# Attention outputs of one unit: written into the output product's PSUM banks instead of the score tiles

## The chip, the cores and the metric

The kernel runs on one core of a Trainium2 chip. The time is device microseconds of one execution, so lower is better. Five engines matter: PE (TensorE: matmuls, and PEld for its weight loads), DVE (VectorE), ACT (ScalarE), POOL (GpSimd) and SP (SyncE, which here only issues DMAs). Each works through its own queue in order and waits on semaphores that the others raise.

## The reference

Attention over 8 batches, 12 heads, 448 positions and a head size of 64, with one more term in the softmax's denominator, followed by a two-layer product whose activation is Mish:

```python
def _attn_ref(q, k, v):
    scale = 1.0 / np.sqrt(q.shape[-1])
    scores = scale * np.matmul(q, k.transpose(0, 1, 3, 2))
    m = np.max(scores, axis=-1, keepdims=True)
    e = np.exp(scores - m)
    attn = e / (np.sum(e, axis=-1, keepdims=True) + np.exp(-m) + 1e-09)
    return np.matmul(attn, v)

def _moe_ref(x, w_in, w_out):          # x: 3584 x 768, w_in: 768 x 2048, w_out: 2048 x 768
    h = x @ w_in
    return (h * np.tanh(np.log1p(np.exp(h)))) @ w_out
```

`x` is the attention output with the heads side by side. The reference guards the exponential for h over 20.

## The kernel before

**Pairs and units.** Heads are handled in pairs: 6 pairs to a batch (`HP`), 48 in all. Three pairs make a unit (`UNIT_PAIRS`), two units a batch, so there are 16 units, numbered from 0. Batch 0 (units 0 and 1) runs through a loop of its own; then one loop goes over units 2 to 19, of which 2 to 15 have attention work. The instructions are put into the engines' queues in exactly the order in which this code calls them.

**A unit of the main loop** has two stages. In the first, twelve steps (numbered 0 to 11, four for each of three pairs) each call `exps` for the scores of this step, then `flush_late`, then some *filler*, then `scores_ahead`. From unit 4 on the filler is the output product (`mm2_part`, line 446) of earlier batches, cut into chunks of two matmuls; the list `weight` says which share of it each step gets (5.2 for the first, 1 for eight, 0.4 for three). In the second stage the input product (`mm1_mish`, line 382) makes eight tiles of 128 hidden columns; between them stand, for the next unit, three groups of transposes of q and k (line 179), their copies out of PSUM (line 210 on DVE for q, into `qd`; line 218 on ACT for k), the sums' reciprocal (lines 296, 300), the multiplies that normalise the three pairs (line 317 on DVE, line 315 on POOL for the third), and the first three score steps.

**Scores.** Seven tiles of 128 query rows make a pair, two to a step, so a pair's steps 0 to 2 do two score matmuls (line 249), one DVE maximum over both banks (line 270, 128 x 896) and two ACT exponentials (line 283), and step 3 does one of each. A score tile has two banks; there are three such tiles, used in turn, so a step's scores wait for the exponentials of three steps before. In step 3 the second bank of the tile is unused.

**Attention outputs.** The normalised exponentials `en` are turned by a DMA transpose (line 321, issued by SP) into `eT`. `av_pair` (line 358) then makes a pair's output with eight matmuls of 112 x 64 weights, accumulated in one bank, and puts a copy into `xT` (line 367) on the list `late`; `flush_late` issues it. The input product of a batch reads `xT`. In units 4 to 15 the three outputs of the unit before are made by `scores`, at step 3 of each pair, in the unused bank of the step's own score tile: `av_with` names the pair, and `bank=sc[:, 1, :]` the place. The output's matmuls so stand just ahead of the step's one score matmul.

**The other banks.** Two single banks, `mo0` and `mo1`, are handed out by `mo_take` and come back when their content has been copied. The output product uses them part by part (384 or 192 columns of 128 rows, sixteen matmuls), its copy to `o_sb` (line 433) is also on `late`; the input product uses them tile by tile, in turn with one bank of the first score tile, and a bank is free when Mish (line 388) has read it.

**What is loaded when.** SP issues the loads of q, k and v, the transposes and the stores of the result; POOL issues the loads of `w_in_sb` and `w_out_sb` (line 148, the last four in unit 4) between its casts of q, k and v (lines 162 to 164).

The step loop, as far as the change touches it:

```python
            exps(idx)
            ...
            flush_late()
            acc += weight[n]
            want = int(total * acc / sum(weight) + 1e-6)
            while done < want:
                fn, w = filler.popleft()
                fn()
                done += w
            scores_ahead(end)
```

Of the kernel before, what the change touches and what calls it, by code (L numbers as in the profile page):

```python
# [15 lines left out]
UNIT_PAIRS = 3  # L16
# [3 lines left out]
def kernel(  # L20
# [28 lines left out]
    STEPS = 4  # L49
# [47 lines left out]
    ]  # L97

    loaded, casted, qkT, att, xT, gT, o_sbs, stats = {}, {}, {}, {}, {}, {}, {}, {}
    av_with, mids = {}, {}  # L100
    late = deque()

    def flush_late():
# [125 lines left out]
    def scores(idx):  # L229

        p, s = divmod(idx, STEPS)
        if s == 0:
            if p < HP or p % UNIT_PAIRS == 0:
                for nm in ("negm", "sums", "expm", "den", "rden"):
                    stats[nm] = st_pool.tile([128, UNIT_PAIRS, NTILE], FP32, tag=nm, name=nm)
            at = 0 if p < HP else p % UNIT_PAIRS
            att[p] = {nm: t[:, at, :] for nm, t in stats.items()}
            att[p].update(en=en_bufs[p % N_EN], whole=dict(stats))
        st = att[p]
        qT, kT = qkT[p]  # L240
        kA, kB = kT[0:64, :], kT[64:128, :]
        sc = sc_tiles[idx % len(sc_tiles)]
        if s == STEPS - 1 and p in av_with:
            av_pair(av_with.pop(p), bank=sc[:, 1, :])
        if p >= DIAG_FROM:
            cols = tuple(range(2 * s, min(2 * s + 2, NTILE)))
            negm = st["negm"][:, cols[0] : cols[-1] + 1]
            for bk, i in enumerate(cols):
                nc.tensor.matmul(  # L249
                    sc[:, bk, 0:S], lhsT=qT[:, i].rearrange("d h r -> d (h r)"), rhs=kT,  # L250
                    start=True, stop=True,
                )
        elif s < 3:
            qa, qb = 128 * s, 64 + 128 * s
            nc.tensor.matmul(  # L255
                sc[:, 0, 0:S], lhsT=qT[0:64, qa : qa + 128], rhs=kA, start=True, stop=True
            )
            nc.tensor.matmul(
                sc[:, 1, 0:S], lhsT=qT[64:128, qb : qb + 128], rhs=kB, start=True, stop=True
            )  # L260
            cols, negm = (s, 4 + s), st["negm"][:, s : s + 5 : 4]
        else:
            nc.tensor.matmul(
                sc[0:64, 0, 0:S], lhsT=qT[0:64, 384:S], rhs=kA, start=True, stop=True
            )
            nc.tensor.matmul(
                sc[64:128, 0, 0:S], lhsT=qT[64:128, 0:64], rhs=kB, start=True, stop=True
            )
            cols, negm = (3,), st["negm"][:, 3:4]
        nc.vector.tensor_reduce(  # L270
            out=negm, in_=sc[:, 0 : len(cols), 0:S], axis=AX.X, op=ALU.max, negate=True
        )
        st["sc", s] = (sc, cols)
# [67 lines left out]

        late.append(evac)

    def av_pair(p, act=False, bank=None):
        b, hp = p // HP, p % HP
        eT = att[p]["eT"]
        v_bf = casted[p][2]
        if b not in xT:
            xT[b] = xT_pool.tile([128, DM_T, S], BF16, tag="xT", name="xT")
        av = mo_take() if bank is None else bank  # L350
        for j in range(NT):
            for h in range(2):
                if p >= DIAG_FROM:
                    by_h = eT[0:SP_, j, :].rearrange("c (i h r) -> c h i r", h=2, r=64)
                    e_h = by_h[:, h]
                else:
                    e_h = eT[0:SP_, j, h * S : (h + 1) * S]
                nc.tensor.matmul(  # L358
                    av[h * 64 : (h + 1) * 64, 0:S],
                    lhsT=v_bf[:, h, j * D : (j + 1) * D],  # L360
                    rhs=e_h,
                    start=(j == 0), stop=(j == NT - 1),
                )
        copy = nc.scalar.copy if act else nc.vector.tensor_copy

        def evac():
            copy(out=xT[b][:, hp, :], in_=av[:, 0:S])  # L367
            if bank is None:
                mo_free.append(av)

        late.append(evac)
        del att[p], casted[p], qkT[p]


    def mm1_mish(b, ff):
        if ff == 0:
# [90 lines left out]
    for g in range(B // 2):  # L467
        u0 = first_mm2 + 4 * g
        rest = plan.pop(u0, [])
        if g == 0:  # L470
            plan[u0] = [(0, i, 0, 2) for i in range(2)] + [(0, 2, 0, 1)]
            plan[u0 + 1] = [(0, 2, 1, 1)] + [(0, i, 2, 2) for i in range(3)]
        else:
            plan[u0] = rest + whole(g, 0) + [(g, 1, 0, 1)]
            plan[u0 + 1] = [(g, 1, 1, 1), (g, 1, 2, 2)] + whole(g, 2)
        plan[u0 + 2] = [(g, 4, 0, 2), (g, 4, 2, 1)] + whole(g, 3)
        plan[u0 + 3] = [(g, 4, 3, 1)] + whole(g, 5) + [(g, 6, 0, 2)]
        if g < B // 2 - 1:
            plan[u0 + 4] = [(g, 6, 2, 2)]
        else:  # L480
            plan[u0 + 3] += [(g, 6, 2, 2)]


    weight = [5.2] + [1.0] * (steps - STEPS) + [0.4] * (STEPS - 1)

    LEAD = UNIT_PAIRS + 1
    LOAD_AT = (0, 3, 6)
    HEAD = HP
# [50 lines left out]

    for u in range(UNITS_PER_B, N_UNITS + 2 * UNITS_PER_B):  # L540
        attn = u < N_UNITS
        filler = deque()
        for part in plan.get(u, []):
            filler.extend(mm2_part(*part))
        total, done, acc = sum(w for _, w in filler), 0, 0.0
        p0 = u * UNIT_PAIRS
        if attn and u >= first_mm2:
            av_with.update({p0 + i: p0 + i - UNIT_PAIRS for i in range(UNIT_PAIRS)})
        end = min((u + 1) * UNIT_PAIRS, N_PAIRS) * STEPS

        for n in range(steps):
            pi, s = divmod(n, STEPS)
            p, idx = p0 + pi, p0 * STEPS + n
            late_tp = u == UNITS_PER_B and n == STEPS
            if late_tp:
                transpose_pair(p0 + 2)
            exps(idx)
            if late_tp:
                evac_qk(p0 + 2)
            if u == UNITS_PER_B + 1:  # L560
                for part in TURN_AT[1].get(n, []):
                    turn_on_pe(*part)
# [8 lines that stand above are left out]
            if n in LOAD_AT:  # L571
                load_pair(p0 + LOAD_AT.index(n) + LEAD)
                cast_pair(p0 + LOAD_AT.index(n) + LEAD - 1)
            if u - UNITS_PER_B < len(AV_AT):
                early = AV_AT[u - UNITS_PER_B]
                if n in early:
                    av_pair(early[n])
                if u == UNITS_PER_B:
                    for part in TURN_AT[0].get(n, []):
                        turn_on_pe(*part)  # L580
            elif s == (2 if pi else 0) and N_PAIRS <= p < N_PAIRS + UNIT_PAIRS:
                av_pair(p - UNIT_PAIRS)
            if u - UNITS_PER_B < len(W_AT):
                load_w(W_AT[u - UNITS_PER_B].get(n, 0))
        assert done == total

        moe = u < N_UNITS + UNITS_PER_B
        b, w = (u - UNITS_PER_B) // UNITS_PER_B, u % UNITS_PER_B
        nxt = p0 + UNIT_PAIRS
        todo = sorted(range(p0, nxt), key=lambda p: p in BY_PE)  # L590
        for f in range(FF_U):
            if moe:
                mm1_mish(b, w * FF_U + f)
            if u == UNITS_PER_B and f in (2, 6):
                load_w(1)
            if not attn:
                continue
            if f == 0:
                denominators(att[p0]["whole"])
                normalise(todo[0], dma=todo[0] not in BY_PE)  # L600
            if f in (1, 3, 5):
                transpose_pair(nxt + f // 2, bank=f // 2 % 2)
                evac_qk(nxt + f // 2)
            if f == 4:
                scores_ahead(min(nxt * STEPS + 1, N_PAIRS * STEPS))
            if f >= FF_U - 2:
                scores_ahead(min(nxt * STEPS + f - FF_U + 4, N_PAIRS * STEPS))
            if f == 3:
                normalise(todo[1], dma=todo[1] not in BY_PE)
            if f == 4:  # L610
                normalise(todo[2], dma=todo[2] not in BY_PE, on_pool=True)
        if moe and w == UNITS_PER_B - 1:
            gather_mid(b)
# [32 lines left out]
```

## Time and profile before

| What | Value |
|---|---|
| median of 3 runs | 487.4 us (486.32 to 488.11) |
| the profiled execution | 486.33 us, of which the span from first to last instruction is 484.6 |
| mean granted TensorE clock | 0.996 of full speed |
| exponentials, line 283 | 336, 209.3 us of ACT, mean 636 ns |
| maxima, line 270 | 192, 182.5 us of DVE; 1085 ns over two banks, 623 ns over one |
| output product, line 446 | 1024 matmuls, 142.1 + 24.9 us of PE |
| input product, line 382 | 768 matmuls, 141.1 + 20.8 us of PE |
| attention outputs, line 358 | 384 matmuls, 34.1 us (288 in score tiles) + 15.0 us (96 in mo banks) of PE |
| their copies, line 367 | 36 from score tiles (DVE, mean 615 ns), 12 from mo banks |

Busy time of PE is the time in which at least one matmul is under way; matmuls follow each other in a pipeline, so a mean of 326 ns for 384 columns goes with a start every 0.1625 us. "Idle before, releaser" says how long an engine stood and which instruction's semaphore came last before it went on. In units 6 to 15 a unit takes 26.3 to 26.6 us.

### The profile page before, as it was taken

How to read it: one execution, taken by the hardware profiler on the slowest of the kernel's cores; microseconds unless marked ns; L12 is line 12 of the kernel's file. 1: busy time of each engine (PE TensorE's matmuls, PEld its weight loads, DVE VectorE, ACT ScalarE, POOL GpSimd, SP SyncE). 2: the span in 40 equal slices, each digit the busy share in tenths (PEclk: the TensorE clock that was granted, in tenths of full speed). 3: DMA queues.
4: the chain of work that ended last, by engine and by line, in shares of the span. 5: the costliest groups of instructions: out<-in, count | busy, mean ns of one | idle time of the engine just before them, and what ended most of it. 6: DMA issues, size and time to landing. Idle time of an engine off the chain costs nothing.

```text
span 484.6 us, 8804 instructions
## 1 busy us (share of the span) xinstructions
PE 448.3 (93%) x2992; PEld 249.0 (51%) x2992; DVE 347.1 (72%) x702; ACT 348.8 (72%) x906; POOL 160.6 (33%) x266
## 2 busy tenths in 40 slices
PE   4566897898999999999999999999999999999996
PEld 2222444455555555555555565555555555556563
DVE  4898987978688786878698887878687868420021
ACT  5989778879786988879797879788797979412300
POOL 4623157355413324353434232343435230300000
PEclk9999998999999999999999999999999999999999
DMA  8999999999999999898998989998989595771112
GB/s 231 199 214 227 243 191 234 221 201 237 182 234 270 203 205 203 226 195 234 191 258 169 237 169 211 203 222 222 179 242 198 155 186 124 147 148 32 34 41 90
DMA packets 209452, 92.19 MB, mean 190 GB/s; under 512 B 166272, under 2 KB 205952, under 8 KB 209408
## 3 DMA queue, kind: packets, MB, share of 16 engines
q1 hardware_dynamic: 201920, 85.35, 81.2%
q0 software_dynamic: 7488, 6.29, 9.0%
q8 instruction: 23, 0.38, 0.3%
q14 instruction: 21, 0.17, 0.1%
HBM read 45.61 MB, written 11.01 MB: 117 GB/s over the span
## 4 chain that ended last, share of the span: by engine, by line
PE 72%; DVE 12%; ACT 7%; DMA 5%; issue 2%; SPq 1%; POOL 0%; DVEq 0%; POOLq 0%
PE mo L446 25%; PE mo L382 24%; PE sc L249 8%; DVE negm L270 7%; ACT en L283 6%; PE sc L358 6%; PE sc L382 3%; PE sc L179 3%; DMA eT<-en 2%; DVE en L317 2%; DMA k_f<-in_k_dram 1%; PE mo L358 1%; DMA q_f<-in_q_dram 1%; PE sc L255 1%; DVE eT L336 1%
## 5 line engine op out<-in xcount | busy, mean ns | idle before, releaser
L283 ACT ACTIVATE en<-sc,negm 128x448 bf16<-128x448 f32 x336 | 209.3, 636 | 26.9 <-DVE negm L270 15.2
L270 DVE TENSOR_REDUCE negm<-sc 128x2 f32<-128x896 f32 x192 | 182.5, 970 | 52.6 <-PE sc L249 42.6
L446 PE MATMUL mo<-w_out_sb,gT 128*128 128x384 bf16 (+1 forms) x896 | 142.1, 303 | 0.0
L382 PE MATMUL mo<-xT,w_in_sb 128*128 128x448 bf16 x672 | 141.1, 352 | 1.0 <-DVE xT L367 0.9
L388 ACT ACTIVATE gT<-mo 128x448 bf16<-128x448 f32 x112 | 61.2, 547 | 77.4 <-PE mo L382 77.1
L446 PEld LDWEIGHTS <-gT 128*128 128x128 bf16 x896 | 84.0, 98 | 46.8 <-issue 1.3
L382 PEld LDWEIGHTS <-w_in_sb 128*128 128x128 bf16 x768 | 72.8, 98 | 63.6 <-issue 2.5
L315 POOL TENSOR_SCALAR en<-en,rden 128x448 bf16<-128x448 bf16 x98 | 61.4, 646 | 114.7 <-DVE rden L308 98.7
L249 PE MATMUL sc<-kT,qd 128*128 128x448 bf16 x252 | 71.5, 354 | 0.3 <-ACT en L283 0.2
L283 ACT ACTIVATION_READ_ACCUMULATOR en<-sc,negm 128x1 f32 x336 | 69.0, 205 | 0.0
L162 POOL CAST q_bf<-q_f 112x512 bf16<-112x512 f32 x47 | 28.9, 615 | 120.1 <-DMA q_f<-in_q_dram 110.5
L317 DVE TENSOR_SCALAR en<-en,rden 128x448 bf16<-128x448 bf16 x238 | 64.2, 343 | 0.9
L433 DVE COPY o_sb<-mo 128x384 f32<-128x384 f32 (+1 forms) x64 | 32.1, 502 | 41.7 <-PE mo L446 41.5
L249 PEld LDWEIGHTS <-qd 128*128 128x128 bf16 x252 | 24.5, 97 | 28.9 <-issue 13.5
L358 PE MATMUL sc<-eT,v_bf 112*64 112x448 bf16 x288 | 34.1, 357 | 3.5 <-ACT en L283 2.3
L164 POOL CAST v_bf<-v_f 112x512 bf16<-112x512 f32 x48 | 29.6, 616 | 16.4 <-DMA v_f<-in_v_dram 13.4
L358 PEld LDWEIGHTS <-v_bf 112*64 112x64 bf16 x384 | 20.9, 114 | 24.9 <-issue 16.9
L210 DVE TENSOR_SCALAR qd<-sc 64x448 bf16<-64x448 bf16 x72 | 27.8, 386 | 6.4 <-PE sc L179 5.9
L255 PE MATMUL sc<-kT,qd 64*128 64x448 bf16 x36 | 17.6, 509 | 15.6 <-ACT en L283 13.3
L163 POOL CAST k_bf<-k_f 112x512 bf16<-112x512 f32 x47 | 28.9, 614 | 8.2 <-DMA k_f<-in_k_dram 7.5
L446 PE MATMUL mo<-w_out_sb,mid 128*128 128x384 bf16 x128 | 24.9, 326 | 0.0
L179 PEld LDWEIGHTS <-q_bf 112*128 112x128 bf16 x192 | 14.5, 104 | 17.8 <-DVE q_bf L162 4.4
(50 smaller groups left out, 311.4 us busy)
## 6 DMA issues: line engine op xcount, KB each, us to landing
q_f<-in_q_dram SPq DMA_DIRECT2D x48, 224.0 KB, 4.9
k_f<-in_k_dram SPq DMA_DIRECT2D x48, 224.0 KB, 5.2
v_f<-in_v_dram SPq DMA_DIRECT2D x48, 224.0 KB, 5.5
w_in_sb<-in_moe_w_in_dram POOLq DMA_DIRECT2D x12, 256.0 KB, 5.8
w_out_sb<-in_moe_w_out_dram POOLq DMA_DIRECT2D x8, 384.0 KB, 8.1
out_dram<-o_sb SPq DMA_DIRECT2D x7, 336.0 KB, 3.4
out_dram<-o_sb SPq DMA_DIRECT2D x8, 288.0 KB, 4.1
out_dram<-o_sb SPq DMA_DIRECT2D x8, 240.0 KB, 3.2
```

The source lines that it names most:

```text
L164: nc.gpsimd.tensor_copy(out=v_bf, in_=v_f)
L179: nc.tensor.transpose(by_s[s][:, t * SP_ : (t + 1) * SP_], src[:, t].rearrange("p h d -> p (h d)"), ident[:SP_, :SP_],)
L249: nc.tensor.matmul(sc[:, bk, 0:S], lhsT=qT[:, i].rearrange("d h r -> d (h r)"), rhs=kT, start=True, stop=True,)
L270: nc.vector.tensor_reduce(out=negm, in_=sc[:, 0 : len(cols), 0:S], axis=AX.X, op=ALU.max, negate=True)
L283: nc.scalar.activation(out=st["en"][:, :, c, 0:SP_], in_=sc[:, bk, 0:S].rearrange("q (j c) -> q j c", j=NT), func=AF.Exp, bias=st["negm"][ ...
L315: nc.gpsimd.tensor_scalar(scalar2=1.0, op0=ALU.mult, op1=ALU.mult, **args)
L317: nc.vector.tensor_scalar(scalar2=None, op0=ALU.mult, **args)
L358: nc.tensor.matmul(av[h * 64 : (h + 1) * 64, 0:S], lhsT=v_bf[:, h, j * D : (j + 1) * D], rhs=e_h, start=(j == 0), stop=(j == NT - 1),)
L382: nc.tensor.matmul(h_ps[:, 0:S], lhsT=w_in_sb[:, dm, ff * 128 : (ff + 1) * 128], rhs=xT[b][:, dm, :], start=(dm == 0), stop=(dm == DM_T - 1),)
L388: nc.scalar.activation(out=gT[b][:, ff, :], in_=h_ps[:, 0:S], func=AF.Mish)
L433: nc.vector.tensor_copy(out=o_sb[:, cols], in_=st["o"][:, 0:n_cols])
L446: nc.tensor.matmul(st["o"][:, 0:n_cols], lhsT=src[:, ff, c0 : c0 + 128], rhs=w_out_sb[:, ff, cols], start=(ff == 0), stop=(ff == FF_T - 1),)
```

## The change

`av_with` and the `bank` argument go. From unit 4 on, in units with attention, the three outputs of the unit before are entries of the filler: each is inserted in the middle of the chunks of one of the unit's first three parts of 384 columns (an entry with weight 6, where a chunk of 384 columns has weight 2 and one of 192 columns weight 1), or stands at the end if there are fewer such parts, as in unit 4. `av_now` makes the output in a bank from `mo_take` and at once issues what is in `late`, its own copy included. In three places of the plan the part of 192 columns comes ahead of the others.

```diff
--- before.py
+++ after.py
@@ -97,7 +97,7 @@
     ]
 
     loaded, casted, qkT, att, xT, gT, o_sbs, stats = {}, {}, {}, {}, {}, {}, {}, {}
-    av_with, mids = {}, {}
+    mids = {}
     late = deque()
 
     def flush_late():
@@ -240,8 +240,6 @@
         qT, kT = qkT[p]
         kA, kB = kT[0:64, :], kT[64:128, :]
         sc = sc_tiles[idx % len(sc_tiles)]
-        if s == STEPS - 1 and p in av_with:
-            av_pair(av_with.pop(p), bank=sc[:, 1, :])
         if p >= DIAG_FROM:
             cols = tuple(range(2 * s, min(2 * s + 2, NTILE)))
             negm = st["negm"][:, cols[0] : cols[-1] + 1]
@@ -341,13 +339,13 @@
 
         late.append(evac)
 
-    def av_pair(p, act=False, bank=None):
+    def av_pair(p, act=False):
         b, hp = p // HP, p % HP
         eT = att[p]["eT"]
         v_bf = casted[p][2]
         if b not in xT:
             xT[b] = xT_pool.tile([128, DM_T, S], BF16, tag="xT", name="xT")
-        av = mo_take() if bank is None else bank
+        av = mo_take()
         for j in range(NT):
             for h in range(2):
                 if p >= DIAG_FROM:
@@ -365,12 +363,15 @@
 
         def evac():
             copy(out=xT[b][:, hp, :], in_=av[:, 0:S])
-            if bank is None:
-                mo_free.append(av)
+            mo_free.append(av)
 
         late.append(evac)
         del att[p], casted[p], qkT[p]
 
+
+    def av_now(p):
+        av_pair(p)
+        flush_late()
 
     def mm1_mish(b, ff):
         if ff == 0:
@@ -468,12 +469,12 @@
         u0 = first_mm2 + 4 * g
         rest = plan.pop(u0, [])
         if g == 0:
-            plan[u0] = [(0, i, 0, 2) for i in range(2)] + [(0, 2, 0, 1)]
+            plan[u0] = [(0, 2, 0, 1)] + [(0, i, 0, 2) for i in range(2)]
             plan[u0 + 1] = [(0, 2, 1, 1)] + [(0, i, 2, 2) for i in range(3)]
         else:
-            plan[u0] = rest + whole(g, 0) + [(g, 1, 0, 1)]
+            plan[u0] = [(g, 1, 0, 1)] + rest + whole(g, 0)
             plan[u0 + 1] = [(g, 1, 1, 1), (g, 1, 2, 2)] + whole(g, 2)
-        plan[u0 + 2] = [(g, 4, 0, 2), (g, 4, 2, 1)] + whole(g, 3)
+        plan[u0 + 2] = [(g, 4, 2, 1), (g, 4, 0, 2)] + whole(g, 3)
         plan[u0 + 3] = [(g, 4, 3, 1)] + whole(g, 5) + [(g, 6, 0, 2)]
         if g < B // 2 - 1:
             plan[u0 + 4] = [(g, 6, 2, 2)]
@@ -483,6 +484,7 @@
 
     weight = [5.2] + [1.0] * (steps - STEPS) + [0.4] * (STEPS - 1)
 
+    AV_WEIGHT = 6
     LEAD = UNIT_PAIRS + 1
     LOAD_AT = (0, 3, 6)
     HEAD = HP
@@ -539,13 +541,17 @@
 
     for u in range(UNITS_PER_B, N_UNITS + 2 * UNITS_PER_B):
         attn = u < N_UNITS
-        filler = deque()
+        p0 = u * UNIT_PAIRS
+        filler, avs = deque(), deque()
+        if attn and u >= first_mm2:
+            avs.extend((lambda p=p: av_now(p), AV_WEIGHT) for p in range(p0 - UNIT_PAIRS, p0))
         for part in plan.get(u, []):
-            filler.extend(mm2_part(*part))
+            chunks = mm2_part(*part)
+            if avs and part[3] == 2:
+                chunks.insert(len(chunks) // 2, avs.popleft())
+            filler.extend(chunks)
+        filler.extend(avs)
         total, done, acc = sum(w for _, w in filler), 0, 0.0
-        p0 = u * UNIT_PAIRS
-        if attn and u >= first_mm2:
-            av_with.update({p0 + i: p0 + i - UNIT_PAIRS for i in range(UNIT_PAIRS)})
         end = min((u + 1) * UNIT_PAIRS, N_PAIRS) * STEPS
 
         for n in range(steps):
```

With it the outputs stand in PE's queue, counted in units 5 to 15, after 24 matmuls of the output product; straight after score step 5; and two product matmuls after score step 9. In DVE's queue their copies stand ahead of the maxima of steps 3, 6 and 10, where before they stood behind those of steps 3, 7 and 11. In unit 4 they stand ahead of score step 3, straight after step 7, and ahead of step 11.

## The prediction

> **What bounds the kernel now.** I read the busy rows first, then the windows of the product stages, then the stage at 183.64 us instruction by instruction, then the landings of the transposes.
>
> ```profile
> PE 448.3 (93%) x2992; PEld 249.0 (51%) x2992; DVE 347.1 (72%) x702; ACT 348.8 (72%) x906; POOL 160.6 (33%) x266
> ```
>
> The mean hides three stages. Columns below: stretch, its length, then busy time of PE, PEld, DVE, ACT, POOL. Each stretch runs from a unit's first output-product matmul to its first input-product matmul.
>
> ```profile
> 183.64:198.59 14.95, 14.95 (x105) 8.46 (x104) 11.06 (x15) 13.77 (x39) 6.19 (x11) 1.00 1.06 250
> 128.94:144.93 15.99, 15.03 (x105) 8.47 (x104) 11.06 (x15) 13.77 (x39) 5.40 (x10) 1.00 1.10 222
> 102.41:117.54 15.13, 12.89 (x89) 7.25 (x88) 11.81 (x16) 13.83 (x41) 8.40 (x15) 1.00 1.04 228
> ```
>
> In unit 7 (183.64), and nearly so in all of units 6 to 15, PE is never idle; ACT is busy 13.77 of 14.95 us. Units 5 (128.94) and 4 (102.41) hold idle PE time. Who waits there (total, times, longest):
>
> ```profile
> ACT en L283 <- DVE xT L367: 8.7, 21, 1.5
> ...
> PE sc L358 <- ACT en L283: 2.3, 4, 0.8
> PE sc L358 <- DMA eT<-en: 1.0, 1, 1.0
> ```
>
> So the attention outputs cost ACT 8.7 us and PE 3.3 us, which looks like the gain on offer. The timeline of unit 7 shows what it is worth:
>
> ```profile
> 187.00 0.95 PE L358 MATMUL sc<-eT,v_bf 112*64 112x448 bf16 x8
> ...
> 188.89 0.62 DVE L367 CAST xT<-sc 128x448 bf16<-128x448 f32 x1
> ...
> 189.62 0.63 ACT L283 ACTIVATE en<-sc,negm 128x448 bf16<-128x448 f32 x1 [0.50 <-DVE xT L367]
> ...
> 199.46 0.63 ACT L283 ACTIVATE en<-sc,negm 128x448 bf16<-128x448 f32 x1
> ...
> 200.87 1.32 DVE L317 TENSOR_SCALAR en<-en,rden 128x448 bf16<-128x448 bf16 x5
> ...
> 201.60 0.54 ACT L388 ACTIVATE gT<-mo 128x448 bf16<-128x448 f32 x1
> ```
>
> The exponential of the shared score tile waits 0.50 for the output's drain, yet PE is paced by a longer chain: last exponential (199.46), sums and reciprocal, seven L317 multiplies, then the qd copy (202.59 to 203.37). PE's second group of transposes starts at 203.52 and needs that copy: a margin of 0.10 us with 0.04 for the hand-over. Likewise the first Mish (201.60 to 202.14) frees a bank that PE takes at 202.39, margin 0.20. If the last exponential comes over 0.1 us later, PE stops.
>
> **The change, part by part.**
>
> *Instructions.* 36 outputs (units 4 to 15) move: 8 matmuls, 8 weight loads, one 0.615 us drain each. None is added or removed on any engine; the drain stays on DVE. Cost 0 in work.
>
> *Entering and leaving an output on PE.* Start to start, the matmul before L358 takes 0.256 (187.00) or 0.278 (191.93) us instead of 0.163, and L358's last pair to the next matmul 0.285. The 0.278 includes a hand-over from ACT: the second and third outputs start 0.04 us after the exponential that frees their score tile. In a mo bank the wait is for an o_sb copy. Elsewhere the entry is 0.176 (160.65). Saving per unit: 0 to 0.2 us; I take 0.04. Leaving into a product row (unit 16, 428.65) costs the same 0.285.
>
> *The plan's order* (192-column parts first): the same parts, 0.0825 us per 192-column and 0.1625 per 384-column matmul. Nothing on the path; if its cover went, one hand-over of 0.04.
>
> *What the outputs now stand before.* The weight of 6 shares the outputs into the twelve steps. The first moves from 3.36 to 2.71 us after the unit's start, the second from 8.29 to 7.24, the third from 13.22 to 12.25. They used to stand before score steps 3, 7 and 11 (one matmul, one 0.62 us maximum); now the second stands before step 6 and the third before step 10 (two matmuls, a 1.08 us maximum), and DVE takes the drain ahead of that maximum. I follow unit 7 through the queues by hand. Durations from its rows: score pair to maximum 0.65, single 0.40; the next DVE instruction starts 1.00 after a double maximum, 0.54 after a single, 0.53 after an xT drain, 0.465 after an o_sb copy; maximum to exponential 0.034 (0.115 if another wait stands ahead); exponentials 0.61 apart (0.62 after a pause); a tile is free 0.77 after its last exponential starts. Start times in us from the unit's start:
>
> | | score 4, exp 4 | score 5, exp 5 | score 6, exp 6 | score 8, exp 8 | score 10, exp 10 | exp 11 |
> |---|---|---|---|---|---|---|
> | before | 5.09, 6.90 | 6.12, 8.36 | 7.15, 9.60 | 10.02, 11.83 | 12.08, 14.53 | 15.82 |
> | after | 5.42, 7.18 | 6.77, 8.53 | 8.12, 10.06 | 10.00, 11.92 | 13.13, 14.91 | 16.14 |
>
> Exp 3 gains (5.98 to 5.39) and exp 4 gives it back, because score 4 stands behind two more product matmuls. Maximum 6 waits for the second drain (8.42 to 8.95), so exp 6 starts at 10.06 and score 9 waits 0.10 on it. The third drain starts at 13.24, maximum 10 at 13.79, exp 10 at 14.91 and exp 11 at 16.14, 0.32 us late. Queued behind it: Mish (bank taken 0.12 late), multiplies, qd copy, second transposes. Less the margin of 0.10, PE stands 0.22 us per unit. With the entry at 0.176 everything shifts and it is 0.06. I take 0.22, since 0.256 is the entry of the first output in seven of these ten units. Ten units: +2.2 us, bounds −2.0 (all entries saved, ACT never last) and +3.2 (no margin).
>
> *Unit 4.* Its three outputs wait 0.8, 1.0 and 0.7 us for ACT; in mo banks they don't. The same steps put exp 11 at 14.62 instead of 15.99, so the unit's second transposes come 1.4 us earlier.
>
> *Unit 5* takes that away.
>
> ```profile
> 121.68 11.62 DMA eT<-en
> ```
>
> (from the chain of waits.) This transpose shares the DMA engines with the last w_out_sb loads, which POOL issues at 115 to 119 us and which land by 129.97; it lands at 133.30, and the first output waits for it. POOL issues these loads after casts that wait for their own loads, not for unit 4. Starting the transpose 1.4 earlier behind the same packets brings 0 to 1.4; I take 0.1. After it, PE now has 0.65 us more product left, and exp 11 comes 1.0 us later from there on (13.43 after that output against 12.45). The normalise row then decides:
>
> ```profile
> 147.21 2.87 DVE L317 TENSOR_SCALAR en<-en,rden 128x448 bf16<-128x448 bf16 x7
> ```
>
> Seven multiplies take 2.87 us here against 1.81 at 119.81, while POOL casts run from 147.77 to 149.70; PE's second transposes wait 0.80 for them. About 0.9 us later they overlap the casts less: 2.6 us. Net, these transposes come 0.6 us later than 150.83; bounds −1.4 and +1.0. [...]
>
> *DMA order and landings.* In unit 7 the three transposes land 2.8, 3.5 and 4.8 us before their outputs; 0.65 to 1.05 us earlier is covered. Without that cover each wait would be PE's.
>
> *Sum.* +2.2 +0.6 = +2.8 us on the profiled execution's 486.33 (span 484.6 and 1.73 around it): 489.1. That execution is the fastest of three; from the median of 487.4 the sum gives 490.2.
>
> **Rivals.** 0.5% is 2.4 us, about what these measurements can tell from no change; the bounds are 484.96 and 489.84.
>
> 1. *Faster: ACT is not the last.* If exp 11 comes no later than before, PE keeps its margin and loses its waits: 0.2 in ten units, 0.7 beyond that in the third outputs at 223, 276 and 329, and unit 4's 1.4: 4.1, so 483.3. For it: ACT loses 8.7 us of waits on drains. Against: ACT is idle only 1.2 us in unit 7, and the table has it pause 1.2 before exp 4 alone. It decides below a lag of 0.1.
>
> 2. *Within 0.5%.* Entries of 0.176 (+0.6 in ten units) and a landing 0.5 earlier in unit 5 (+0.2): 488.2. Table entries are good to about 0.1 us and the margin is 0.10, so this is near.
>
> 3. *Much slower: the two mo banks.* The third output takes the bank drained by the o_sb copy ending at 12.20, 0.05 before it. If DVE is 0.5 late there, score 10, exp 10 and exp 11 follow: +0.7 per unit, 494.4. For it: no slack in the table. Against: the copies are DVE's 0.55 us rows, with no POOL partner. [...]
>
> 4. *It moves, but nothing follows*, PE being full: 487.4.
>
> **How the numbers follow.** Forecast 0.42 and rival 3 0.08: slower 0.50. Rival 2 0.28 and rival 4 0.04: same 0.32. Rival 1: 0.18. The time is the forecast's, 490.2, its own range 489.8 to 491.8. The 8-in-10 range, with the unknown entries, margin and landing, reaches 485.5 to 492.5.
>
> **What would show it.** Right: the rows of ACT waiting for xT gone; ACT waiting for negm grown; in units 6 to 15 PE waits of 0.1 to 0.3 us at the second transposes (on qd) or the fourth input-product group (on a Mish); the unit period up from 26.4 to about 26.6. Unit 4's product stage near 13.5 us instead of 15.1; the first output of unit 5 still starting near 133.3, after a longer wait. Wrong: last exponentials no later than 15.8 after the unit's start, or a period under 26.4; or output waits on o_sb (rival 3).

## The result and the profile after

| | before | changed |
|---|---|---|
| median of 6 runs, us | 487.75 (486.32 to 489.06) | 492.14 (490.58 to 493.79) |
| profiled execution, us (span) | 486.33 (484.6) | 493.79 (492.0) |
| mean granted TensorE clock | 0.996 | 0.964 |

The ratio is 1.009, with a 95% interval of 1.0066 to 1.0113: slower, by 4.4 us between the medians, where 2.8 was forecast. The forecast's own range (489.8 to 491.8) ends 0.3 us below the 492.14; its wide one (485.5 to 492.5) takes it in. The profiled executions stand 7.4 us apart. From the starts of the units' stages in the two traces, that difference is made of:

| stretch | before, us | changed, us | difference |
|---|---|---|---|
| start to unit 4's first output product | 102.41 | 105.15 | +2.74 |
| from there to unit 6's first input product | 69.82 | 71.70 | +1.88 |
| nine units from there, to unit 15's first input product | 237.96 | 239.93 | +1.97 |
| the rest | 74.41 | 75.22 | +0.81 |

The first row isn't the change's: no output moves before unit 4. Every kernel of this document has the same code up to there, and this stretch takes 101.80 to 106.33 us in their fourteen traces; what spreads it isn't known. The clock rows of the two pages (40 slices of the span, tenths of full speed) differ in slices 4 to 6, but that doesn't explain it. First the kernel before:

```profile
PEclk9999998999999999999999999999999999999999
```

The changed kernel, with its busy row; slice 12 (135 to 148 us) will matter:

```profile
PE 452.6 (92%) x2992; PEld 247.4 (50%) x2992; DVE 350.5 (71%) x702; ACT 348.8 (71%) x906; POOL 161.6 (33%) x266
...
PEclk9996588999989999999999999999999999999999
```

The kernel before runs at half rate there as well. Eight matmuls of an output take it 1.71 us up to 62 us of the span and 0.95 from there on:

```profile
60.27 1.71 PE L358 MATMUL mo<-eT,v_bf 112*64 112x448 bf16 x8
...
62.40 0.95 PE L358 MATMUL mo<-eT,v_bf 112*64 112x448 bf16 x8
```

Its trace holds no record of the clock from before its first change to full rate at 62 us, and the row shows such a stretch as full. The changed kernel reached the full rate once before, from 37.1 to 40.5 us, so that its row shows the half rate behind it. Most of the difference between the mean clocks of 0.996 and 0.964 is this. Experiment 7's row is like the changed kernel's, and unit 4's first output product starts at 102.67 us.

The other three rows add up to 4.66 us, near the 4.4 of the medians. They too are one execution each, and the second is the least sure: in experiment 5, with no output moved, it is 68.41 us. The third is firm: 237.93 to 238.36 us in the three kernels with the outputs in the score tiles (before, experiment 5, the second of experiment 8), 239.59 to 239.94 in the four with all of them moved as here, unit 5 apart (the changed one, experiments 6 and 7, the first of 8). The windows of the changed kernel for units 7, 5 and 4, columns as in the prediction (the last three are granted clock, DMA share, GB/s):

```profile
188.43:203.45 15.02, 15.02 (x105) 8.33 (x104) 11.82 (x16) 13.36 (x39) 6.40 (x11) 1.00 1.06 250
130.96:150.15 19.19, 16.59 (x105) 8.73 (x103) 11.82 (x16) 13.46 (x39) 5.79 (x10) 0.91 1.10 230
105.15:118.71 13.56, 12.79 (x88) 6.76 (x87) 11.95 (x17) 13.30 (x39) 6.86 (x12) 1.00 0.93 216
```

Unit 4's stage is 1.57 us shorter, unit 5's 3.20 longer, with a granted clock of 0.91 where before it had 1.00. The waits of the changed kernel (total, times, longest):

```profile
ACT en L281 <- DVE negm L268: 32.7, 49, 4.0
...
PE mo L356 <- DMA eT<-en: 3.1, 2, 2.6
```

ACT's 8.7 us of waits for the outputs' copies are gone, and its wait for the maxima has grown from 15.2 to 32.7. ACT is as busy as before (348.8 us): it got its time back in one place and lost it in another. Unit 7 shows where, in the timeline of the changed kernel (start, length, engine, what; in brackets the idle time before it and its releaser):

```profile
195.85 1.09 DVE L268 TENSOR_REDUCE negm<-sc 128x2 f32<-128x896 f32 x1 [0.26 <-PE sc L247]
...
196.86 0.61 DVE L365 CAST xT<-mo 128x448 bf16<-128x448 f32 x1
...
197.39 2.78 DVE L268 TENSOR_REDUCE negm<-sc 128x2 f32<-128x896 f32 x3
...
203.35 0.63 ACT L281 ACTIVATE en<-sc,negm 128x448 bf16<-128x448 f32 x1 [0.34 <-DVE negm L268]
...
204.59 0.63 ACT L281 ACTIVATE en<-sc,negm 128x448 bf16<-128x448 f32 x1
```

The second output's copy (196.86) stands ahead of maximum 6. Counted from the unit's start at 188.43, the exponentials 4, 5, 6, 8, 10 and 11 start at 7.19, 8.55, 10.07, 11.92, 14.92 and 16.16; the prediction's table had 7.18, 8.53, 10.06, 11.92, 14.91 and 16.14.

### The profile page after: what moved, and what is told of

It reads as the page before. It is cut to its first block, busy times and chain, and to the rows that moved or that the text cites. A ratio compares the mean times of both kernels' runs of the same rounds, so it can differ in the third digit from the quotient of the medians.

```text
span 492.0 us, 8718 instructions
## 1 busy us (share of the span) xinstructions
PE 452.6 (92%) x2992; PEld 247.4 (50%) x2992; DVE 350.5 (71%) x702; ACT 348.8 (71%) x906; POOL 161.6 (33%) x266
## 4 chain that ended last, share of the span: by engine, by line
PE 73%; DVE 10%; DMA 7%; ACT 6%; issue 2%; SPq 1%; POOL 0%; DVEq 0%; POOLq 0%
PE mo L447 26%; PE mo L383 22%; PE sc L247 9%; PE mo L356 7%; ACT en L281 5%; DVE negm L268 4%; DMA eT<-en 4%; DVE en L315 3%; PE sc L179 3%; PE sc L383 3%; DMA k_f<-in_k_dram 1%; DMA q_f<-in_q_dram 1%; PE mo L330 1%; PE sc L253 1%; DVE xT L365 1%
## 5 line engine op out<-in xcount | busy, mean ns | idle before, releaser
L281 ACT ACTIVATE en<-sc,negm 128x448 bf16<-128x448 f32 x336 | 209.3, 637 | 34.2 <-DVE negm L268 32.7
L447 PEld LDWEIGHTS <-gT 128*128 128x128 bf16 x896 | 82.7, 98 | 49.5 <-issue 6.2
L315 DVE TENSOR_SCALAR en<-en,rden 128x448 bf16<-128x448 bf16 x238 | 64.4, 342 | 0.9
L434 DVE COPY o_sb<-mo 128x384 f32<-128x384 f32 (+1 forms) x64 | 32.1, 502 | 37.1 <-PE mo L447 36.6
L356 PE MATMUL mo<-eT,v_bf 112*64 112x448 bf16 x384 | 49.6, 385 | 3.1 <-DMA eT<-en 3.1
L365 DVE CAST xT<-mo 128x448 bf16<-128x448 f32 x45 | 27.8, 621 | 29.5 <-PE mo L356 29.0
L247 PEld LDWEIGHTS <-qd 128*128 128x128 bf16 x252 | 22.8, 98 | 26.6 <-issue 12.5
L356 PEld LDWEIGHTS <-v_bf 112*64 112x64 bf16 x384 | 19.0, 115 | 27.6 <-issue 18.1
```

What stands on the lines that cost most here:

```text
L247: nc.tensor.matmul(sc[:, bk, 0:S], lhsT=qT[:, i].rearrange("d h r -> d (h r)"), rhs=kT, start=True, stop=True,)
L281: nc.scalar.activation(out=st["en"][:, :, c, 0:SP_], in_=sc[:, bk, 0:S].rearrange("q (j c) -> q j c", j=NT), func=AF.Exp, bias=st["negm"][ ...
L315: nc.vector.tensor_scalar(scalar2=None, op0=ALU.mult, **args)
L356: nc.tensor.matmul(av[h * 64 : (h + 1) * 64, 0:S], lhsT=v_bf[:, h, j * D : (j + 1) * D], rhs=e_h, start=(j == 0), stop=(j == NT - 1),)
L434: nc.vector.tensor_copy(out=o_sb[:, cols], in_=st["o"][:, 0:n_cols])
L447: nc.tensor.matmul(st["o"][:, 0:n_cols], lhsT=src[:, ff, c0 : c0 + 128], rhs=w_out_sb[:, ff, cols], start=(ff == 0), stop=(ff == FF_T - 1),)
```

## The experiments

Each kernel was timed in five rounds beside the kernel before on the same chip; a ratio is to that. The runs with outputs at other places come first, then unit 5, then both together.

**1. Second and third outputs before single maxima.**

```diff
-                chunks.insert(len(chunks) // 2, avs.popleft())
+                at = len(chunks) // 2 if len(avs) == UNIT_PAIRS else 3 * len(chunks) // 4
+                chunks.insert(at, avs.popleft())
```

> The changed kernel with one thing moved: the second and third output of a unit stand after three quarters of their part instead of the middle, so that in units 5 to 15 they come straight before score steps 7 and 11 (one maximum of 0.62 us) and not before steps 6 and 10 (two banks, 1.08 us). Banks and early drains stay. Theory (the place in the score chain makes the exponentials late): the unit period goes from 26.6 back to about 26.4, the waits of 0.1 us on a Mish, on qd and of step 9 on ACT vanish, and the time falls by 10 x 0.24 = 2.4 us to 489.7. Rival (two banks are too few): the period stays at 26.6 and the time at 492.

489.4 us, ratio 1.0032 (1.0008 to 1.0055). The changed kernel's window of unit 7's output product is shown above (15.02 us); its input product's follows:

```profile
203.45:215.02 11.57, 11.57 (x79) 6.45 (x78) 9.37 (x27) 8.42 (x19) 3.29 (x6) 1.00 0.82 180
```

and both windows of unit 7 in this kernel:

```profile
188.01:202.92 14.91, 14.91 (x104) 8.34 (x103) 11.79 (x16) 13.60 (x39) 6.18 (x11) 1.00 1.05 247
202.92:214.33 11.41, 11.41 (x81) 6.46 (x79) 9.38 (x27) 7.99 (x19) 3.44 (x7) 1.00 0.86 193
```

The unit takes 26.32 us instead of 26.59. (Before: 14.95 and 11.40, 26.35.) The whole loss of the steady units is in the place of two outputs, and it splits as the prediction's two waits do: 0.11 in the first stage, 0.16 in the second.

**2. Third output alone.**

```diff
+                at = 3 * len(chunks) // 4 if len(avs) == 1 else len(chunks) // 2
+                chunks.insert(at, avs.popleft())
```

> The changed kernel with the third output of each unit alone at three quarters of its part (before a single maximum); the second stays in the middle, before a double one. The hand table of the prediction has the second output put exponential 8 only 0.09 us late and the third put exponential 11 0.32 late. Theory (it is the third whose place costs): the steady unit returns to 26.4 us and the time to about 490. Rival (the second output's place, which delays exponential 6, is the loss): 26.6 us a unit, 492.

489.42 us, ratio 1.004 (1.0017 to 1.0063). The same two windows of this kernel:

```profile
187.68:202.70 15.02, 15.02 (x105) 8.33 (x103) 11.82 (x16) 13.70 (x40) 6.39 (x11) 1.00 1.09 242
202.70:214.10 11.40, 11.40 (x79) 6.46 (x78) 9.38 (x27) 7.88 (x19) 3.28 (x6) 1.00 0.90 199
```

The second stage is back at 11.40, the first still 15.02. The unit takes the 26.42 us of the theory, but the loss has two parts: the third output's place costs the 0.17 of the input product (Mish and second transposes late), and the second output's place the 0.11 of the output product, where score step 9 waits for exponential 6.

**3. The banks without the places.** The kernel before with its outputs in the free bank, at their old places, first with the copy left on `late`, then drained at once.

```diff
-            av_pair(av_with.pop(p), bank=sc[:, 1, :])
+            av_pair(av_with.pop(p))
```

> The kernel before with the outputs at their old places but in mo banks instead of the score tiles, their copies issued a step later as before. Theory: the exponential of step 3, 7 and 11 no longer waits for the copy (ACT waiting for xT, 8.7 us, gone), but the next part wants the output's bank 0.65 to 1.0 us after the output, before the late copy has ended: PE waits 0.4 us twice and 0.8 once in a unit, some 1.6 x 11 = 18 us at most, 495 to 505. So new banks need the early copy. If banks cost nothing: 487 or less.

506.27 us, ratio 1.0385 (1.0361 to 1.0409), just above the 495 to 505 that were expected. Waits of this kernel:

```profile
PE mo L382 <- DVE xT L367: 7.1, 13, 0.6
PE mo L446 <- DVE xT L367: 4.8, 19, 0.9
```

The copy stands behind maxima, and PE stops for the bank it holds, both in the output product and at the first input product.

```diff
+            av_pair(av_with.pop(p))
+            flush_late()
```

> The kernel before with its outputs in the output product's free bank, at their old places (ahead of the last score step of each pair), each drained at once. This is the bank without the place. Theory (the place ahead of a double maximum costs, the bank does not): the steady unit stays at 26.4 us instead of 26.6, unit 4 keeps its gain, unit 5 waits for its transpose as in the changed kernel: 488 to 490. Rival (the exchange of two banks between outputs and product groups is what costs): the period grows to 26.8 or more, 492 and up.

493.17 us, ratio 1.0116 (1.0083 to 1.0149). The time fits the rival, the trace doesn't. The steady period is 26.3 to 26.4 us, as the theory had it, but two units (8 and 12) take 29.2 and 29.0, and the step from unit 4's to unit 5's input product takes 3.4 us more than before (4.0 in the changed kernel). Unit 8 in this kernel's timeline:

```profile
219.80 0.81 PE L447 MATMUL mo<-w_out_sb,gT 128*128 128x384 bf16 x4
222.03 0.95 PE L359 MATMUL mo<-eT,v_bf 112*64 112x448 bf16 x8 [1.42 <-DVE o_sb L434]
```

There the output comes four matmuls into a part and takes the bank of the part before, whose copy is still behind maxima. This is the mechanism of the prediction's third rival. In the middle of a part, as the change has it, the third output also goes on an `o_sb` copy, but enters in the usual 0.255 us.

**4. The copy behind the maximum**, in the changed kernel:

```diff
     def av_now(p):
         av_pair(p)
-        flush_late()
```

> The changed kernel with each output's drain left to the next step's start, behind the maximum that the changed kernel puts it ahead of. Theory (the double maximum comes late mainly because its scores stand behind two more product matmuls, and the drain's 0.53 us is the other part; a bank held longer costs PE something): steady period 26.5 to 26.7, time 491 to 492.5. Rival A (the drain ahead of the maximum is the whole steady loss): 26.4, 489.7. Rival B (the held bank stops PE, as it did at the old places): 27 or more, 495 and up.

503.72 us, ratio 1.0321 (1.0295 to 1.0346): rival B. Its waits:

```profile
PE mo L446 <- DVE xT L365: 6.6, 11, 0.6
PE mo L382 <- DVE xT L365: 4.2, 13, 0.7
```

With two banks, the copy has to come at once; that it stands ahead of a maximum is the price. Experiment 1 picks the cheaper maximum.

**5. The plan's order alone**, in the kernel before (192-column parts first).

```diff
-            plan[u0] = [(0, i, 0, 2) for i in range(2)] + [(0, 2, 0, 1)]
+            plan[u0] = [(0, 2, 0, 1)] + [(0, i, 0, 2) for i in range(2)]
...
-            plan[u0] = rest + whole(g, 0) + [(g, 1, 0, 1)]
+            plan[u0] = [(g, 1, 0, 1)] + rest + whole(g, 0)
...
-        plan[u0 + 2] = [(g, 4, 0, 2), (g, 4, 2, 1)] + whole(g, 3)
+        plan[u0 + 2] = [(g, 4, 2, 1), (g, 4, 0, 2)] + whole(g, 3)
```

> The kernel before with only the changed order of the plan (192-column parts first), outputs in the score tiles as before. Theory: no effect, 487.75 +- 0.5. Rival (the order of parts shifts stores and loads on SP and costs in the last units): 488.5 or more, with the last units longer.

488.29 us, ratio 1.0012 (0.999 to 1.0033): nothing that can be told from no change. Its clock row has the low digits of slices 4 to 6 too, in a kernel whose outputs all stand where they stood; unit 4's first output product starts at 105.67 us.

**6. Unit 5's first output one part later.**

```diff
-            if avs and part[3] == 2:
+            if avs and part[3] == 2 and (u != first_mm2 + 1 or part != (0, 0, 2, 2)):
```

> The changed kernel, in unit 5 alone with each output one part later, so that PE reaches the first about 2.6 us later and does more product matmuls before it. Theory (the transpose of unit 5 lands late, PE stands 2.9 us for it, and the granted clock falls for some 3 us afterwards): the wait goes from 2.8 to under 0.5 us, no half-rate matmuls after it, and the time falls by 1.5 to 3 us to about 490. Rival (the chain after it, through maxima and normalising, is what counts in unit 5): within 0.5 us of 492.

489.91 us, ratio 1.0048 (1.0028 to 1.0068). The changed kernel's timeline at unit 5:

```profile
130.96 2.78 PE L447 MATMUL mo<-w_out_sb,gT 128*128 128x192 bf16 x24
136.35 1.70 PE L356 MATMUL mo<-eT,v_bf 112*64 112x448 bf16 x8 [2.60 <-DMA eT<-en]
137.98 1.46 PE L447 MATMUL mo<-w_out_sb,gT 128*128 128x384 bf16 x4
```

and this kernel's:

```profile
131.54 4.41 PE L447 MATMUL mo<-w_out_sb,gT 128*128 128x192 bf16 x34
...
137.42 0.95 PE L356 MATMUL mo<-eT,v_bf 112*64 112x448 bf16 x8
```

In the changed kernel PE stands 2.60 us, and then an output of eight matmuls takes 1.70 us instead of 0.95, and four product matmuls 1.46 instead of 0.81: half the rate, until about 139.5. Here the transpose lands no earlier, 31.1 us after unit 4's first output product in both (136.74 less 105.62 here, 136.30 less 105.15 there), but PE has work until then, the granted clock stays at 1.00, and the same output takes 0.95. So it is PE's pause that brings the half rate, not the place in the program or the late transpose. Units 4 to 6 (the second row of the table above) take 68.67 us, below the 69.82 of before, while the steady units stay at 26.6.

**7. PE kept busy in the wait.** Which part of unit 5's loss is the wait, and which the rate behind it?

```diff
         av = mo_take()
+        if p == first_mm2 * UNIT_PAIRS:
+            for _ in range(14):
+                nc.tensor.matmul(av[:, 0:S], lhsT=w_in_sb[:, 0, 0:128],
+                                 rhs=w_in_sb[:, 1, 0:S], start=True, stop=True)
```

> The changed kernel with 14 matmuls of 448 columns (2.6 us at full rate, on weights, into the bank that the output then overwrites) ahead of unit 5's first output: PE works while it waits for the transpose. The matmuls add nothing to the result. Theory (it is PE's pause of 2.8 us that halves its rate for the 3 us behind it): the output still starts when its transpose lands, but its matmuls and the product's behind it run at full rate (192 columns in 0.08, 384 in 0.16 us), and the stage from the first output-product matmul to the first input-product matmul shrinks from 19.2 to about 17.6 us: 492.1 less 1.6, 490.5. Rival (the clock drops whatever PE does, or the exponentials set the pace behind the wait): stage 19 us, time 492.

491.72 us, ratio 1.0066 (1.0043 to 1.009). Unit 5 in this kernel's timeline:

```profile
131.20 2.81 PE L351 MATMUL mo<-w_in_sb 128*128 128x448 bf16 x14
133.94 0.95 PE L360 MATMUL mo<-eT,v_bf 112*64 112x448 bf16 x8
134.82 0.50 PE L451 MATMUL mo<-w_out_sb,gT 128*128 128x384 bf16 x2
```

and its window:

```profile
128.58:146.25 17.67, 17.67 (x119) 9.71 (x117) 11.83 (x16) 13.46 (x39) 5.80 (x10) 1.00 1.11 236
```

The stage takes 17.67 us where 17.6 was expected, at a granted clock of 1.00, though the output starts 0.8 us after its transpose landed (133.13), since the fourteen matmuls ran on. Counted from the stage's start, the output starts as late as in the changed kernel (5.36 us, there 5.39), so what is left of the difference, 1.5 us, is the price of the half rate. That the pause causes it is shown by experiment 6, not here: this execution's transpose would have held PE for only 1.9 us, and a pause as long kept the full rate in experiment 4. The median came down less than that (by the two ratios 1.2 us, and the intervals overlap): the stage is what shows it.

**8. The last four loads of `w_out_sb` ahead of unit 4's casts**, in the changed kernel and in the kernel before.

```diff
-    W_AT = ({5: 1, 9: 1}, {1: 1, 4: 1, 5: 1, 7: 1, 9: 1, 11: 1}, {3: 1, 5: 1, 7: 1, 9: 1})
+    W_AT = ({5: 1, 9: 1}, {1: 1, 4: 1, 5: 1, 7: 1, 9: 1, 11: 1}, {0: 4})
```

> The changed kernel with one edit: the last four w_out_sb loads of unit 4, which GpSimd issues two by two behind casts (at 118 and 122 us), are all issued at the unit's first step, ahead of the second and third pair's casts. Theory (these loads share the DMA engines with unit 5's first transpose, so its output waits, and the long pause of PE then halves its rate for some us): the issue of that transpose shrinks from 9.8 to about 5 us, PE's wait of 2.77 us before unit 5's first output goes below 0.5, and the granted clock there stays full: 492.1 less 2.8 less some 1.7 of the half-rate stretch, about 487.8. Rival (the transpose is late on its own, or behind the loads of q, k and v, and the clock drops for another reason): the wait stays above 2 us, time 491 to 492.

490.32 us, ratio 1.006 (1.0032 to 1.0089); 487.8 was expected. Its windows of units 5 and 4:

```profile
130.83:146.33 15.50, 15.04 (x104) 8.49 (x103) 12.14 (x17) 13.39 (x39) 6.46 (x11) 1.00 1.09 238
104.30:118.57 14.27, 12.71 (x89) 6.76 (x88) 11.99 (x17) 14.01 (x41) 7.34 (x12) 1.00 1.15 182
```

The wait of 2.6 us and the low clock are gone, as the theory had it, but less came of it. The first transpose of unit 5 still takes 7.8 us to issue (9.8 in the changed kernel, about 4.3 for the two behind it), and a transpose of unit 4 is now late: its third output waits 1.01 us. That transpose takes 10.4 us from issue to landing (107.01 to 117.44) where the changed kernel's takes 6.1: it now runs beside the moved loads, and the wait went with them. Units 4 to 6 take 69.67 us, 2.0 less than in the changed kernel.

> The kernel before with the four w_out_sb loads ahead of unit 4's casts and nothing else. Theory: its PE wait of 1.0 us for unit 5's transpose goes, and the multiplies of that unit may start earlier: 487.8 less 1.0, 486.8, at most 486. If the loads alone were the whole gain of the run with both repairs, this kernel would come out as low as that run: that run should be lower than this one by about the 1.5 us of unit 4.

488.04 us, ratio 1.001 (0.9984 to 1.0035), where a gain of 1.0 us was expected. In its trace PE no longer waits before unit 5's first output, and units 4 to 6 take 69.27 us against 69.82; half a microsecond is less than the medians can tell.

**9. Both repairs.** Experiment 1 with the loads of experiment 8, and experiment 1 with the place of experiment 6.

> Both together: the second and third outputs of a unit at three quarters of their part (before single maxima), and the last four w_out_sb loads ahead of the casts of unit 4. Theory: the two losses are apart (0.24 us a unit in ten units; the wait of unit 5 with its low clock), so both go: 489.4 less 3 to 4.5, about 485.6, below the kernel before (487.8), and with it the gain of unit 4 is left. Rival (the losses share a cause, so the second repair brings nothing on top): 488 to 489.5.

486.7 us, ratio 0.9979 (0.9961 to 0.9997), where 485.6 was expected. Unit 4's third output waits in this kernel too, 1.71 us.

> Two repairs that moved the time one at a time, together: second and third outputs at three quarters of their part, and unit 5's first output one part later. Theory: the two losses are apart, so steady units at 26.4 us, no wait of 2.8 us in unit 5, and unit 4's gain of 1.4 kept: 489.9 less 2.4 is 487.5, or by the run with the loads moved 486.7; so 486.5 to 487.5, not slower than before (487.8). Rival (they share a cause): 489.4 or more.

486.25 us, ratio 0.996 (0.9941 to 0.998). Its windows of units 5 and 7:

```profile
132.32:148.09 15.77, 15.07 (x105) 8.41 (x104) 11.92 (x17) 14.28 (x41) 3.94 (x7) 1.00 1.07 230
186.73:201.64 14.91, 14.91 (x105) 8.34 (x103) 11.79 (x16) 13.62 (x39) 6.07 (x11) 1.00 1.05 247
```

The two losses are apart, and with both repaired the moved outputs are 0.4% faster than the kernel before. This is the lowest ratio of all the runs; its interval overlaps that of the other pair of repairs.

## Why the prediction came out as it did

- *Instructions and plan order at nothing*: right. The plan's order alone moved nothing that can be told (experiment 5).
- *Entry and exit of an output*: the saving of 0.04 us per unit came out near. With the places repaired the steady unit takes 26.32 us against 26.35. Of its parts, the second entry gained nothing (0.28 before and after) and the third 0.02; the rest of the 0.03 isn't traced.
- *Steady units, +2.2*: right, with its mechanism. Nine units lost 1.97 us, 0.22 each. Experiments 1 and 2 remove the loss by moving two outputs. The waits are those named: score 9 on exponential 6 (0.11), the Mish bank (0.08), the second transposes on the qd copy (0.10). The working holds too: exponential 11 came 0.34 us late, and less the margin of 0.10 that is the 0.24 by which unit 7 grew (26.59 against 26.35). The wait at score 9 is inside this figure, which counts from the unit's start. But it doesn't hang on exponential 11, as the sum has it: with the third output's place repaired it is still there (experiment 2).
- *Unit 4, 1.4 us earlier*: half right. Its first stage ends 1.57 us sooner, but the second transposes come only 0.7 earlier (19.35 us after the unit's start, 20.06 before): the multiplies of the normalisation took longer. They now run beside POOL's last cast (121.11 to 121.73) and its issue of two loads (121.67 to 123.15), and that this is the cause is read from the times alone. The changed kernel's row:

```profile
121.26 2.48 DVE L315 TENSOR_SCALAR en<-en,rden 128x448 bf16<-128x448 bf16 x7
```

  It took 1.81 before, and PE waits 0.83 us for the second transposes (their start to start, less a matmul). In unit 5 the same row went from 2.87 to 1.81 (2.6 was forecast), with no cast beside it.
- *Unit 5, net +0.6*: the step that failed. That the transpose would land no earlier was right: it is issued at 123.80 and lands at 136.30, 0.26 us later than before once the 2.74 us of the start are taken off. But "after it, PE now has 0.65 us more product left" counted that product at full rate. PE's wait of 2.6 us brought the half rate, 1.5 us by experiment 7. Units 4 to 6 lost 1.88 in all; without the 1.5 that is 0.4, beside the forecast 0.6, and one execution's 1.88 is good to about 1 us.
- *Tail*: forecast at nothing, measured +0.81. Of that 0.27 is unit 15's input product, which waits 0.31 for a Mish bank and belongs to the steady term. The other 0.5 is unit 16, whose third output now waits for its transpose (the prediction looked at the landings in unit 7 alone). In experiment 7's trace, with the same outputs, it doesn't wait. The changed kernel:

```profile
437.95 0.95 PE L356 MATMUL mo<-eT,v_bf 112*64 112x448 bf16 x8 [0.50 <-DMA eT<-en]
```

- *Rivals.* That ACT isn't the last (faster) fell with the table: exponential 11 came 0.34 us late. That two banks don't suffice is real at the old places and with a late copy (experiments 3 and 4: +2.7 and +2.5 us in two units, and 16 to 18 us in all with a late copy), and the middle of a part avoids it. The releases by `o_sb` that were to show it are there, at no cost. The `o_sb` copies of 384 columns take 0.547 to 0.558 us in the kernel before (line 433), beside POOL's work as away from it.

In sum: 2.2 + 0.6 was forecast; 2.24 for the steady units, 0.38 for units 4 to 6 without the half rate, 1.5 for the half rate and 0.54 for unit 16 were measured, 4.66 in all. That this ends so near the medians' 4.4 is partly luck, as the stretches of single executions vary by more.

## What to carry to other kernels

When work moves in a full queue, write down which instructions of the next engine stand behind it: here the same output cost 0.1 to 0.2 us ahead of a maximum over two banks and nothing ahead of a maximum over one. Where a change lengthens a wait of PE, read the granted clock behind it: here every pause of 2.2 us or more came with 3.4 or 6.8 us at 0.50, and in unit 5 that cost 1.5 us beside the wait itself (experiment 7). Count it in the price, or give PE something to do until then. Waits for a landing are checked at every place where the moved instruction occurs, not in one steady unit alone.

## What the hardware showed

Behind some pauses PE's granted clock fell to 0.50, for 3.4 us or twice that. This is read from the traces behind their first stretch at half rate, which ends at 62.3 us in the kernel before and at 64.4 in the changed one. The pauses, start to start less one matmul, and what came with them:

| kernel | pause, us | granted clock |
|---|---|---|
| before, unit 5 | 1.1 | 1.00 |
| before, batch 0, up to 88.26 | 1.6 | 1.00 |
| experiment 3 (copy on `late`), batch 0, up to 91.33 | 1.6 | 0.50 from 91.82 to 95.24 |
| experiment 9 (loads), unit 4 | 1.9 | 1.00 |
| experiment 4, unit 5 | 1.9 | 1.00 |
| all fourteen traces, batch 0 | 2.2 | 0.50 for 3.4 or 6.8 us |
| experiment 2, unit 5 | 2.5 | 0.50 from 136.69 to 140.10, one output later |
| changed, unit 5 | 2.8 | 0.50 from 136.11 to 139.52 |
| experiment 3 (drained at once), unit 5 | 2.8 | 0.50 from 134.26 to 137.67 |
| experiment 1, unit 5 | 2.9 | 0.50 from 134.56 to 141.38 |
| experiment 7, unit 5 | none | 1.00 |

The kernel before has the pause of batch 0 here, and the window behind it:

```profile
78.11 0.35 PE L263 MATMUL sc<-kT,qd 64*64 64x448 bf16 x1 [2.07 <-ACT en L283]
```

```profile
79.38:82.80 3.42, 3.42 (x21) 2.01 (x21) 3.16 (x5) 3.23 (x11) 1.58 (x3) 0.50 1.11 256
```

The window of unit 5 in experiment 1, with 6.8 us at half rate, has the lowest granted clock of unit 5's windows:

```profile
129.56:150.29 20.73, 18.03 (x105) 9.27 (x103) 11.79 (x16) 13.71 (x39) 6.88 (x12) 0.84 1.09 239
```

The half rate lasted 3.42 us in the kernel before (79.38 to 82.80), 3.41 in the changed kernel's unit 5, and 6.82 in the changed kernel's batch 0 (81.50 to 88.32). It came at no fixed distance from the pause: 1.3 us behind its end in the kernel before (78.11), 0.2 ahead of its end in the changed kernel's unit 5 (136.35), and an output later in experiment 2. It came with every pause of 2.2 us or more in the table, with neither of the two of 1.9 us, and with one of the two of 1.6 us. The length of one pause does not decide alone, since the two of 1.6 us stand at the same place in the program; what else decides was not shown.
